# The opening of an FNet and channel-mix kernel: index patterns, transfers and float32 rows in another order, one angle operation on ScalarE, mu rows on VectorE

## The chip, the cores and the metric

The kernel runs on one core of a Trainium2 chip. The metric is the device time of one execution in microseconds (us). A core has five engines with instruction streams of their own: TensorE (PE in the profile; PEld is its weight load), VectorE (DVE), ScalarE (ACT), GpSimd (POOL) and SyncE (SP). They wait for each other through semaphores. Transfers are issued by SP, ScalarE and GpSimd on queues of their own and are carried out by 16 DMA engines.

## What is computed

`x` has 8 batches of 3072 rows of 256 numbers. The first half is the real part of a two-dimensional Fourier transform of each batch, the second a channel mix of that result with its own predecessor row:

```python
X = np.fft.fft(x, axis=1)
X = np.fft.fft(X, axis=2)
x = X.real
x_prev = np.concatenate([zeros, x[:, :-1, :]], axis=1)
xk = mu_k * x + (1.0 - mu_k) * x_prev
xr = mu_r * x + (1.0 - mu_r) * x_prev
k = np.maximum(xk @ w_k, 0.0)
v = k * k @ w_v
r = 1.0 / (1.0 + np.exp(-(xr @ w_r)))
return r * v
```

`w_k` is 256 x 1024, `w_v` 1024 x 256, `w_r` 256 x 256. Inputs and output are float32; the kernel computes in float16 with float32 sums.

## The kernel before

**The transform** is made of matmuls with tables of sines. A row and its mirror image in the batch have related coefficients, so the kernel first *folds*: `fold` (L160) adds rows read forwards (`xp`) to mirrored rows (`xm`) and writes `p` in float16, on VectorE. A batch has two halves: half 0 has nine slots of 96 rows (slot 0 by itself), half 1 has eight. `xp` comes by plain strided transfers (`load_p`, L129), which turn float32 into float16 on the way; `xm` comes by gathers (`load_m`, `load_m0`, L143 to L151), whose row numbers are in `idx_8`, `idx_4` and `idx_0`. These are patterns that GpSimd writes with `iota`. A gather is issued by GpSimd after its pattern is there. GpSimd's queue carries all transfers into SBUF but one: batch 0's first five slots, which SP loads as float32 into `xp_32` (L245) without a change of type.

**Batch 0** is the opening, since nothing runs before it. It folds in pieces: slots 1 to 4 of half 0, then slots 5 to 8, then half 1 in two pieces of four, then slot 0 (L900 to L916). `a_sum` (L616) multiplies each piece by the table `w_pm`, four matmuls of 208 columns per pair of slots; ScalarE or VectorE copies the sums out of PSUM into `a`. Then come the second factor (`d_units`, L643), a correction (`turned`, L685), the third factor with the table `m_cs` (`c_sums`, L704), and the mix with mu. The first matmuls of the channel mix are at L818.

**The tables** are made on the chip while the first rows are on their way: GpSimd writes `ramp` and `pcol_i`, VectorE makes rows from them, TensorE multiplies these into angles in PSUM, VectorE scales and reduces them (`ts`, L307, is its helper; `m_angles`, L430), and ScalarE takes the sine. `m_angles` writes `ang` for c = 0 and 1: a block of 32 columns and a block of 416 each, from PSUM to int32, then one AND over all 896. `m_sine` (L462) makes `m_cs` from it; `m_turned` (L466) copies it with a sign on VectorE. `w_pm` is written by ScalarE (L425, L427), and two operations of VectorE scale a part of it and make its negative (L894, L895).

**mu** is a row of 256 numbers for each of two uses. `mu_rows` (L255) puts it into the order that the kernel needs with three small copies on ScalarE; two small matmuls (L906) turn it into columns, which ScalarE copies into `muf_t`. The first mix and `turn_table` read them.

**Order.** Each engine runs its instructions in the order in which the program emits them; the last line, `pin_order`, fixes it. `keep_busy` (L232) fills waiting time of TensorE with matmuls of zeros; `NF` says how many in each place (`NF[0]` in front of the first `a_sum`). The weights `w_k` are gathered by `loads` (L475) behind the transfers of batch 0, with row numbers that `rows` (L271) writes on GpSimd.

Of the kernel before, what the change touches and what calls it, by code (L numbers as in the profile page):

```python
# [39 lines left out]
def kernel(  # L40
# [10 lines left out]
    nc = tc.nc  # L51
# [60 lines left out]
    p_sb = [const.tile([112, 256 * (9 - h) + 2], FP16, name=f"p{h}") for h in range(2)]  # L112
    xp_32 = const.tile([96, 5, 256], FP32)
    idx_4 = const.tile([96, 2], UINT32)
    idx_8 = const.tile([96, B, 2], UINT32)
    idx_0 = const.tile([96, B], UINT32)
    idx_g8 = const.tile([112, B, 2], UINT32)
# [10 lines left out]

    def load_p(b, h, q0=0):  # L129
        r, n = 9 * h + q0, 9 - h - q0  # L130
        if b > 1:
            for g in range(2):
                src = dataclasses.replace(x[b, 32 * g + r:32 * g + r + 1, :],
                                          ap=[[64 * D, N1], [D, n], [1, D]])
                nc.gpsimd.dma_start(out=xp_t[b, h][64 * g:64 * g + N1, 0:n], in_=src)
            return
        src = dataclasses.replace(x[b, r:r + 1, :], ap=[[32 * D, 96], [D, n], [1, D]])
        nc.gpsimd.dma_start(out=xp_t[b, h][0:96, q0:q0 + n], in_=src)

# [20 lines left out]
    def fold(b, h, q0=0, n=0):  # L160

        n = n or 9 - h
        if (b, h) not in p_t:
            p_t[b, h] = p_sb[h][:, 0:256 * (9 - h)].rearrange("p (q d) -> p q d", d=256)
        k = parts(b)
        p, xp, xm = p_t[b, h][0:k], xp_t[b, h][0:k], xm_t[b, h][0:k]
        o = XM0 + 256 * (8 - h - q0)
        if (b, h, q0) == (0, 0, 0):
            xm, o = xm_00, 1
        if (b, h) == (0, 0) and q0 < 5:  # L170
            xp = xp_32
        V.tensor_tensor(out=p[:, q0:q0 + n], in0=xp[:, q0:q0 + n],  # L172
                        in1=_v(xm, o + 256, [(-256, n), (-1, 256)]), op=ALU.add)
        V.tensor_tensor(out=p[:, q0:q0 + n, 0], in0=xp[:, q0:q0 + n, 0],
                          in1=_v(xm, o, [(-256, n)]), op=ALU.add)
# [56 lines left out]
    def keep_busy(n, ps, cols=512):  # L232

        for _ in range(n):
# [5 lines left out]
    keep_busy(1, fill, 384)  # L240
    NF = (14, 0, 1, 3, 0, 0, 0)

    nc.sync.dma_start(out=xp_32, in_=dataclasses.replace(x[0, 0:1, :],  # L245
                                                         ap=[[32 * D, 96], [D, 5], [1, D]]))
    mu_row = const.tile([2, 257], FP32)
# [7 lines left out]
    def mu_rows():  # L255
        nc.scalar.activation(out=mu_row[:, 256:257], in_=mu_row[:, 128:129], func=AF.Copy)
        for a in range(2):
            nc.scalar.activation(out=mu_p[:, a], in_=_v(mu_row, 256 * a, [(1 - 2 * a, 2),
                                                                         (2 - 4 * a, 64)]),
                                 func=AF.Copy)  # L260

    for h in range(2):
        x_tiles(0, h)
    load_p(0, 0, 5)
    for xm in xm_sb:
# [21 lines left out]
    iota(pcol_i, pattern=[[0, 1]], base=0, channel_multiplier=1)  # L287
    iota(idx_8, pattern=[[S // 8, B], [-1, 2]], base=S // 8 - 1, channel_multiplier=-4)
    iota(idx_4, pattern=[[-1, 2]], base=S // 4 - 3, channel_multiplier=-8)
    load_m(0, 0, 0, 8, idx_8[:, 0, 0:1])  # L290
    load_p(0, 1)
    load_m(0, 1, 1024, 4, idx_4[:, 0:1])
    load_m(0, 1, 0, 4, idx_4[:, 1:2])
    iota(idx_0, pattern=[[S, B]], base=S, channel_multiplier=-32)
    iota(idx_0[0:1], pattern=[[S, B]], base=0, channel_multiplier=0)
    rows()
    load_m0(0)

# [131 lines left out]
    def m_angles():  # L430
        for c in range(2):
            ts(ang[:, c, 0], ang_ps[:, 0:32], float(TURN) / S, MUL, ph_c[:, 2 * c + 1:2 * c + 2],
               ADD)
        rest = ang_ps[:, 32:32 * NJ]
        for c in range(2):
            ts(ang[:, c, 1:], rest, float(TURN) / S, MUL, ph_c[:, 2 * c:2 * c + 1], ADD)
        ts(ang, ang, TURN - 1, ALU.bitwise_and)

# [177 lines left out]
    def a_sum(b, h, i0, eng="A", m=4):  # L616
# [5 lines left out]
        for i in range(m):  # L622
            parts = [(h, i0 + i + 1 - h, 0, 2 * WA, 0, 1)]
            if h and i0 + i == 7:
                parts = [(0, 0, 0, WA, WA, 1), (1, 7, 1, WA, 1, 2)]
            for half, q, o, n, w, step in parts:
# [264 lines left out]


    mu_rows()
    ts(w_pm[:, 0:2, WA:WA + WB], w_pm[:, 0:2, WA:WA + WB], math.sqrt(0.5), MUL)  # L894
    ts(w_pm[:, 2], w_pm[:, 0], -1.0, MUL)  # L895
    m_sine()
# [5 lines left out]
    fold(0, 0, 5, 4)  # L902
    a_sum(0, 0, 4)
    mu_ps = ps_v()
    for a in range(2):
# [4 lines left out]
    nc.scalar.activation(out=muf_t, in_=mu_ps[:, 0:6], func=AF.Copy)  # L910
    m_turned()
    keep_busy(NF[2], ang_ps)
# [295 lines left out]
```

## Time and profile before

| | |
|---|---|
| median of 3 runs | 427.2 us (427.09 to 427.3) |
| the profiled execution | 427.09 us |
| its span, from the first to the last instruction | 425.3 us |
| granted TensorE clock, mean over the span | 1.000 |
| TensorE busy | 419.0 us (99%) |
| VectorE busy | 371.0 us (87%) |
| ScalarE busy | 325.8 us (77%) |
| GpSimd busy | 64.0 us (15%) |

The profile is of one execution. A page of it tells how long each engine was busy, the chain of work that ended last, and the costliest groups of instructions. Further views of the same trace are the timeline of an engine (start, length, engine, line, operation, output<-inputs, shape; in square brackets the idle time before it and what ended it), the chain in order of time, the groups by form, and the DMA queues in a stretch of time. L172 is line 172 of the kernel. The release of a wait is inferred from semaphores. For a transfer that GpSimd issues, the row on GpSimd is the time in which it writes the descriptors; the data move later.

### The profile page before, as it was taken

To read this page: it belongs to the slowest core of one execution; us is meant where nothing else is said; L and a number is where in the kernel's file an instruction comes from. 1 tells how busy PE (TensorE), PEld (TensorE's weight loads), DVE (VectorE), ACT (ScalarE), POOL (GpSimd) and SP (SyncE) were. 2 spreads that over 40 slices of the span, in tenths; PEclk is the share of its full clock that TensorE was granted. 3 is DMA by queue.
4 is the path that set the end of the run, shared out by engine and by line. 5 is a ranking of instruction groups with operands and counts; after the bars stand their busy time and mean duration, and the time that the engine had idled before them with its cause. 6 is when DMAs were issued, how large, how long until landed. Compare 5 with 4: busy or idle time off the path is not lost.

```text
span 425.3 us, 9647 instructions
## 1 busy us (share of the span) xinstructions
PE 419.0 (99%) x3992; PEld 294.1 (69%) x3992; DVE 371.0 (87%) x591; ACT 325.8 (77%) x406; POOL 64.0 (15%) x99
## 2 busy tenths in 40 slices
PE   8999999999999999999999999999999999999996
PEld 3667766776677767776767776777767766776765
DVE  8999999999998989989899898988899776977553
ACT  7889886797867986689767887678876798666661
POOL 7478500200060001400041000500000000000000
PEclk9999999999999999999999999999999999999999
DMA  8879962632385233932349232772323222332333
GB/s 171 111 114 201 229 148 55 116 90 55 70 160 137 54 75 56 219 96 51 76 77 218 57 71 58 135 167 62 70 57 76 55 63 60 74 72 53 76 76 99
DMA packets 35104, 42.08 MB, mean 99 GB/s; under 512 B 4114, under 2 KB 31092, under 8 KB 35060
## 3 DMA queue, kind: packets, MB, share of 16 engines
q1 hardware_dynamic: 27488, 25.41, 24.6%
q0 software_dynamic: 7264, 15.80, 21.7%
q8 instruction: 31, 0.51, 0.5%
q10 hardware_dynamic: 308, 0.26, 0.2%
q14 instruction: 13, 0.11, 0.1%
HBM read 32.08 MB, written 25.17 MB: 135 GB/s over the span
## 4 chain that ended last, share of the span: by engine, by line
PE 96%; DMA 1%; DVE 1%; issue 0%; POOL 0%; ACT 0%; POOLq 0%
PE psW L818 39%; PE psV L859 37%; PE psW L845 10%; PE psV L871 3%; PE psW L739 2%; PE psW L610 1%; DMA xm<-in_x_dram,idx 1%; PE psW L672 1%; PE psW L628 1%; PE psW L650 1%; DVE p L172 0%; PE psW L707 0%; PE psV L628 0%; PE psV L650 0%; PE psW L235 0%
## 5 line engine op out<-in xcount | busy, mean ns | idle before, releaser
L828 ACT ACTIVATE rl<-psW 128x1024 f16<-128x1024 f32 x192 | 193.7, 1031 | 82.3 <-PE psW L818 81.2
L818 PE MATMUL psW<-x,wk 128*128 128x512 f16 (+1 forms) x776 | 193.4, 377 | 0.3 <-DVE x L952 0.3
L859 PE MATMUL psV<-wv_sb,k 128*128 128x256 f16 x1424 | 184.3, 273 | 0.0
L859 PEld LDWEIGHTS <-k 128*128 128x128 f16 x1424 | 136.4, 98 | 38.3
L838 DVE TENSOR_TENSOR k<-rl 128x2048 f16<-128x2048 f16 (+1 forms) x100 | 115.6, 1156 | 26.3 <-ACT rl L828 26.0
L818 PEld LDWEIGHTS <-wk 128*128 128x128 f16 x776 | 75.6, 98 | 54.9 <-issue 0.4
L881 DVE SCALAR_TENSOR_TENSOR o<-psV,r 128x512 f32<-128x512 f32 (+1 forms) x97 | 65.8, 681 | 15.0 <-PE psV L859 14.1
L783 DVE TENSOR_TENSOR x<-y,t 128x1536 f16<-128x1536 f16 (+3 forms) x76 | 62.4, 827 | 2.2
L850 ACT ACTIVATE r<-psW 128x1024 f16<-128x1024 f32 x48 | 49.4, 1030 | 0.8 <-PE psW L845 0.8
L845 PE MATMUL psW<-wr,x 128*128 128x256 f16 x384 | 49.8, 273 | 0.0
L845 PEld LDWEIGHTS <-x 128*128 128x128 f16 x384 | 37.5, 98 | 14.2 <-issue 0.2
L567 ACT ACTIVATE g_all<-psW 128x512 f16<-128x512 f32 (+8 forms) x62 | 28.8, 538 | 1.3 <-PE psW L672 1.0
L567 ACT ACTIVATE a<-psW 128x832 f16<-128x832 f32 x31 | 25.4, 865 | 1.6 <-PE psW L610 1.2
L487 POOL IOTA gate<- 1x1 int32 x7 | 0.8, 121 | 162.5 <-DVE gate L486 162.5
L567 ACT ACTIVATE pq<-psW 128x1024 f16<-128x1024 f32 (+1 forms) x27 | 23.3, 916 | 1.5 <-PE psW L739 1.4
L141 POOL DMA_INDIRECT xm<-in_x_dram,idx_g x18 | 23.1, 1282 | 5.5 <-issue 5.5
L172 DVE TENSOR_TENSOR p<-xp,xm 112x2304 f16<-112x2304 f16 (+6 forms) x19 | 21.6, 1139 | 0.4 <-DMA xm<-in_x_dram,idx 0.4
L772 DVE TENSOR_SCALAR t<-d,muf_t 128x1536 f16<-128x1536 f16 (+3 forms) x44 | 21.9, 509 | 0.1
L772 DVE TENSOR_SCALAR t<-d,mu_m 128x1536 f16<-128x1536 f16 x32 | 19.6, 613 | 0.0
L752 DVE TENSOR_TENSOR y<-pq 128x960 f16<-128x960 f16 (+3 forms) x28 | 15.8, 606 | 3.2 <-ACT pq L567 2.8
L760 DVE TENSOR_TENSOR d<-y 128x1664 f16<-128x1664 f16 (+5 forms) x19 | 16.8, 882 | 0.3 <-ACT y L567 0.2
L871 PE MATMUL psV<-wv_sb,k 128*128 128x256 f16 x112 | 14.7, 273 | 0.0
(148 smaller groups left out, 217.4 us busy)
## 6 DMA issues: line engine op xcount, KB each, us to landing
out_dram<-o SPq DMA_DIRECT2D x189, 128.0 KB, 2.4
xp<-in_x_dram POOLq DMA_DIRECT2D x12, 216.0 KB, 4.3
xp<-in_x_dram POOLq DMA_DIRECT2D x13, 192.0 KB, 6.7
xp<-in_x_dram POOLq DMA_DIRECT2D x2, 384.0 KB, 6.8
wv_sb<-in_moe_w_v_dram POOLq DMA_DIRECT2D x1, 512.0 KB, 7.4
xp<-in_x_dram SPq DMA_DIRECT2D x1, 480.0 KB, 4.3
xp<-in_x_dram POOLq DMA_DIRECT2D x1, 432.0 KB
xm<-in_x_dram,idx_g POOLq DMA_INDIRECT x18, 8.2
```

What stands on the lines that cost most here:

```text
L141: nc.gpsimd.indirect_dma_start(dst, None, src, bass.IndirectOffsetOnAxis(ap=idx, axis=0))
L567: nc.scalar.activation(out=out_ap, in_=in_ap, func=AF.Copy)
L772: V.tensor_scalar(out=dst, in0=src, scalar1=mu, scalar2=None, op0=ALU.mult)
L783: V.tensor_tensor(out=_v(x_t[b, j, m], o, [(64 * step, hi - lo), (step, 64)]), in0=y_t[b][:, lo + 3 * m:hi + 3 * m, a], in1=x_t["t", a][:, ...
L818: nc.tensor.matmul(out=st["k", ds][:, 512 * hs + lo:512 * hs + hi], lhsT=wk_sb[m][a][:, 128 * fc:128 * fc + 128], rhs=xk[:, a, 512 * i + l ...
L828: nc.scalar.activation(out=st["rl"][:, 2 * ds:2 * ds + 2], in_=st["k", ds].rearrange("p (f t) -> p f t", f=2), func=AF.Relu, bias=0.0, sca ...
L838: V.tensor_tensor(out=k2_t[c][:, lo:hi], in0=r, in1=r, op=ALU.mult)
L845: nc.tensor.matmul(out=ps[:, 256 * tb:256 * tb + 256], lhsT=x_t[b, 1, m][:, a, 512 * i + 128 * tb: 512 * i + 128 * tb + 128], rhs=wr_sb[m] ...
L850: nc.scalar.activation(out=st["r", c], in_=ps, func=AF.Sigmoid)
L859: nc.tensor.matmul(out=st["v", tb - h][:, 256 * h:256 * h + 256], lhsT=k2_t[c][:, fc, 128 * tb:128 * tb + 128], rhs=wv_sb[:, fc], start=(f ...
L871: nc.tensor.matmul(out=st["v", tb - h][:, 256 * h:256 * h + 256], lhsT=k2_t[c][:, fc, 128 * tb:128 * tb + 128], rhs=wv_sb[:, fc], start=fc ...
L881: V.scalar_tensor_tensor(out=o.rearrange("p a b -> p (a b)")[:, 0:256 * n], in0=st["v", t0][:, 0:256 * n], scalar=16.0, in1=st["r", c][:, ...
```

## The change

It touches the opening alone.

1. **Which rows come as float32.** SP loads four slots (5 to 8) into `xp_32` instead of five (0 to 4). GpSimd loads slots 0 to 4 with the change of type instead of 5 to 8. So the fold of slots 1 to 4 reads float16, that of 5 to 8 float32, that of slot 0 float16.
2. **GpSimd's order.** Before: xp of half 0, `ramp`, `pcol_i`, `idx_8`, `idx_4`, gather of half 0, xp of half 1, two gathers of half 1, `idx_0` (two patterns), six row patterns, gather of slot 0. After: `ramp`, `pcol_i`, `idx_8`, xp of half 0, gather of half 0, xp of half 1, `idx_4`, first gather of half 1, `idx_0` (two patterns), second gather of half 1, gather of slot 0, six row patterns. `idx_8` and `idx_0` hold two batches instead of eight (4 and 2 columns instead of 16 and 8).
3. **Angles.** The 416-column operation of c = 1 goes from VectorE to ScalarE (Identity with scale and bias). The AND is split into two of 448 columns; between them stand the two operations on `w_pm`, which came behind the AND before.
4. **mu rows.** The three copies go from ScalarE to VectorE, and from in front of `m_sine` to behind the second fold and `m_turned`, in front of the first fold of half 1. `m_turned` keeps its place on VectorE.
5. **Filler and matmuls.** `NF[0]` is 12 instead of 14. In the last piece of half 1 the two matmuls that read slot 0 come behind the two that read half 1.

```diff
-    xp_32 = const.tile([96, 5, 256], FP32)
+    xp_32 = const.tile([96, 4, 256], FP32)
     idx_4 = const.tile([96, 2], UINT32)
-    idx_8 = const.tile([96, B, 2], UINT32)
-    idx_0 = const.tile([96, B], UINT32)
+    idx_8 = const.tile([96, 2, 2], UINT32)
+    idx_0 = const.tile([96, 2], UINT32)
...
-    def load_p(b, h, q0=0):
-        r, n = 9 * h + q0, 9 - h - q0
+    def load_p(b, h, n=0):
+        r, n = 9 * h, n or 9 - h
...
-        p, xp, xm = p_t[b, h][0:k], xp_t[b, h][0:k], xm_t[b, h][0:k]
+        p, xp, xm = p_t[b, h][0:k], xp_t[b, h][0:k, q0:], xm_t[b, h][0:k]
...
-        if (b, h) == (0, 0) and q0 < 5:
+        if (b, h, q0) == (0, 0, 5):
             xp = xp_32
...
-    NF = (14, 0, 1, 3, 0, 0, 0)
+    NF = (12, 0, 1, 3, 0, 0, 0)
...
-    nc.sync.dma_start(out=xp_32, in_=dataclasses.replace(x[0, 0:1, :],
-                                                         ap=[[32 * D, 96], [D, 5], [1, D]]))
+    nc.sync.dma_start(out=xp_32, in_=dataclasses.replace(x[0, 5:6, :],
+                                                         ap=[[32 * D, 96], [D, 4], [1, D]]))
...
     def mu_rows():
-        nc.scalar.activation(out=mu_row[:, 256:257], in_=mu_row[:, 128:129], func=AF.Copy)
+        V.tensor_copy(out=mu_row[:, 256:257], in_=mu_row[:, 128:129])
         for a in range(2):
-            nc.scalar.activation(out=mu_p[:, a], in_=_v(mu_row, 256 * a, [(1 - 2 * a, 2),
-                                                                         (2 - 4 * a, 64)]),
-                                 func=AF.Copy)
+            V.tensor_copy(out=mu_p[:, a], in_=_v(mu_row, 256 * a, [(1 - 2 * a, 2),
+                                                                   (2 - 4 * a, 64)]))
...
-    load_p(0, 0, 5)
...
     iota(ramp, pattern=[[1, P]], base=0, channel_multiplier=0)
     iota(pcol_i, pattern=[[0, 1]], base=0, channel_multiplier=1)
-    iota(idx_8, pattern=[[S // 8, B], [-1, 2]], base=S // 8 - 1, channel_multiplier=-4)
-    iota(idx_4, pattern=[[-1, 2]], base=S // 4 - 3, channel_multiplier=-8)
+    iota(idx_8, pattern=[[S // 8, 2], [-1, 2]], base=S // 8 - 1, channel_multiplier=-4)
+    load_p(0, 0, 5)
     load_m(0, 0, 0, 8, idx_8[:, 0, 0:1])
     load_p(0, 1)
+    iota(idx_4, pattern=[[-1, 2]], base=S // 4 - 3, channel_multiplier=-8)
     load_m(0, 1, 1024, 4, idx_4[:, 0:1])
+    iota(idx_0, pattern=[[S, 2]], base=S, channel_multiplier=-32)
+    iota(idx_0[0:1], pattern=[[S, 2]], base=0, channel_multiplier=0)
     load_m(0, 1, 0, 4, idx_4[:, 1:2])
-    iota(idx_0, pattern=[[S, B]], base=S, channel_multiplier=-32)
-    iota(idx_0[0:1], pattern=[[S, B]], base=0, channel_multiplier=0)
+    load_m0(0)
     rows()
-    load_m0(0)
...
         rest = ang_ps[:, 32:32 * NJ]
-        for c in range(2):
-            ts(ang[:, c, 1:], rest, float(TURN) / S, MUL, ph_c[:, 2 * c:2 * c + 1], ADD)
-        ts(ang, ang, TURN - 1, ALU.bitwise_and)
+        ts(ang[:, 0, 1:], rest, float(TURN) / S, MUL, ph_c[:, 0:1], ADD)
+        nc.scalar.activation(out=ang[:, 1, 1:], in_=rest, func=AF.Identity, bias=ph_c[:, 2:3],
+                             scale=float(TURN) / S)
+        ts(ang[:, 0], ang[:, 0], TURN - 1, ALU.bitwise_and)
+        ts(w_pm[:, 0:2, WA:WA + WB], w_pm[:, 0:2, WA:WA + WB], math.sqrt(0.5), MUL)
+        ts(w_pm[:, 2], w_pm[:, 0], -1.0, MUL)
+        ts(ang[:, 1], ang[:, 1], TURN - 1, ALU.bitwise_and)
...
-                parts = [(0, 0, 0, WA, WA, 1), (1, 7, 1, WA, 1, 2)]
+                parts = [(1, 7, 1, WA, 1, 2), (0, 0, 0, WA, WA, 1)]
...
-    mu_rows()
-    ts(w_pm[:, 0:2, WA:WA + WB], w_pm[:, 0:2, WA:WA + WB], math.sqrt(0.5), MUL)
-    ts(w_pm[:, 2], w_pm[:, 0], -1.0, MUL)
     m_sine()
...
     a_sum(0, 0, 4)
+    m_turned()
+    mu_rows()
     mu_ps = ps_v()
...
     nc.scalar.activation(out=muf_t, in_=mu_ps[:, 0:6], func=AF.Copy)
-    m_turned()
     keep_busy(NF[2], ang_ps)
```

More of the change, by code (lines that the diff above doesn't have):

```diff
@@ L137, in load_p @@
         src = dataclasses.replace(x[b, r:r + 1, :], ap=[[32 * D, 96], [D, n], [1, D]])
-        nc.gpsimd.dma_start(out=xp_t[b, h][0:96, q0:q0 + n], in_=src)
+        nc.gpsimd.dma_start(out=xp_t[b, h][0:96, 0:n], in_=src)
     def gather(dst, src, idx):
@@ L169, in fold @@
             xm, o = xm_00, 1
-        if (b, h) == (0, 0) and q0 < 5:
+        if (b, h, q0) == (0, 0, 5):
             xp = xp_32
-        V.tensor_tensor(out=p[:, q0:q0 + n], in0=xp[:, q0:q0 + n],
+        V.tensor_tensor(out=p[:, q0:q0 + n], in0=xp[:, 0:n],
                         in1=_v(xm, o + 256, [(-256, n), (-1, 256)]), op=ALU.add)
-        V.tensor_tensor(out=p[:, q0:q0 + n, 0], in0=xp[:, q0:q0 + n, 0],
+        V.tensor_tensor(out=p[:, q0:q0 + n, 0], in0=xp[:, 0:n, 0],
                           in1=_v(xm, o, [(-256, n)]), op=ALU.add)
```

## The prediction

> **What bounds the kernel now.** I read the page's shares and its chain first, then the chain of waits of the first 16 us, then the timelines of VectorE, GpSimd, TensorE and ScalarE over that stretch, and last the DMA view in narrow windows.
>
> ```profile
> PE 419.0 (99%) x3992; PEld 294.1 (69%) x3992; DVE 371.0 (87%) x591; ACT 325.8 (77%) x406; POOL 64.0 (15%) x99
> ...
> PE 96%; DMA 1%; DVE 1%; issue 0%; POOL 0%; ACT 0%; POOLq 0%
> ```
>
> TensorE carries 96% of the chain, so the other 4% is where an opening can gain. Of this chain, over the opening (start, length, what):
>
> ```profile
> 1.25 0.20 POOL xp L138
> ...
> 2.79 4.99 DMA xm<-in_x_dram,idx
> ...
> 7.81 1.23 DVE p L172
> ...
> 9.29 1.68 PE psW L628 x16
> ...
> 11.56 0.32 PE psV L235
> 11.88 0.73 PE psW L628 x8
> 12.61 1.05 PE psV L628 x10
> ...
> 18.01 1.03 PE psW L818 x8
> ```
>
> The mirrored rows of batch 0 (first gather) land at 7.79 and release the first fold. From 9.29 the chain names TensorE, though part of that is filler. VectorE shows what really ends last:
>
> ```profile
> 5.01 0.29 DVE L309 TENSOR_SCALAR ueo<-ueo 128x256 int32<-128x256 int32 x1
> 5.22 1.52 DVE L309 TENSOR_SCALAR rl<-psV,ph_c 128x32 int32<-128x32 f32 x4
> 6.77 0.63 DVE L309 TENSOR_SCALAR rl<-rl 128x896 int32<-128x896 int32 x1
> 7.32 0.42 DVE L309 TENSOR_SCALAR w_pm<-w_pm 128x104 f16<-128x104 f16 x2
> 7.81 1.22 DVE L172 TENSOR_TENSOR p<-xp,xm 96x1024 f16<-96x1024 f32 x1
> ...
> 9.94 0.44 DVE L309 TENSOR_SCALAR m_cs<-m_cs,sc 128x896 f16<-128x896 f16 x1
> 10.75 0.69 DVE L172 TENSOR_TENSOR p<-xp,xm 96x1024 f16<-96x1024 f16 x1 [0.37 <-DMA xm<-in_x_dram,idx]
> ```
>
> The first column is the start, the second the length. Two things to see. VectorE finished its table work at 7.32 + 0.42 = 7.74, just before the gather landed: both were critical at once. And the third fold, at 10.75, came after 0.37 us of waiting for the second gather. Its two halves feed the matmuls of 11.7 and 12.6, and from there every stage hangs on the one before, up to the first matmul of the channel mix at 18.01. So the change is worth what it moves that third fold; after that I count 1:1.
>
> **The gathers, the first term.** GpSimd issues its transfers in its own order (a DMA row is its descriptor work, not the transfer):
>
> ```profile
> 1.25 0.68 POOL L138 DMA_DIRECT2D xp<-in_x_dram  x1 [0.81 <-POOLq L1192]
> 2.02 0.28 POOL L286 IOTA ramp<- 128x128 int32 x1
> ...
> 2.29 0.22 POOL L288 IOTA idx<- 96x16 uint32 x1
> 2.43 0.17 POOL L289 IOTA idx<- 96x2 uint32 x1
> 2.79 1.01 POOL L141 DMA_INDIRECT xm<-in_x_dram,idx  x1 [0.19 <-DVE g_i L309]
> ...
> 4.67 0.95 POOL L141 DMA_INDIRECT xm<-in_x_dram,idx  x1 [0.30 <-issue]
> ...
> 11.53 0.94 POOL L141 DMA_INDIRECT wk<-in_moe_w_k_dram,row_i  x1 [0.30 <-issue]
> ```
>
> After the change GpSimd starts with three patterns. If they start at 1.25 as the DMA did: 0.1 for its set-up (1.93 to 2.02), 0.27 from the first to the third start (2.02 to 2.29), 0.17 for a third pattern of 4 columns (the row with 2 takes that), 0.1 to the DMA. The xp transfer is issued at 1.25 + 0.64 = 1.89, 0.64 later than now, and ends at 2.5; 0.30 of gap, and the first gather is issued at 2.8, as now. What the smaller and the later pattern save is spent on having xp between. If the patterns can start sooner (the profile doesn't explain the 0.81 of idle time before the DMA), all this is earlier; half of those 0.81, 0.4, is the most that I allow.
>
> What counts is when the data moves. SP's transfer (queue 1) and GpSimd's (queue 0) share the 16 engines. In the windows 1.2 to 3.6 and 3.6 to 4.4 us:
>
> ```profile
> q1 hardware_dynamic: 89, 0.46, 72.1%
> ```
> ```profile
> q0 software_dynamic: 58, 0.12, 78.3%
> q1 hardware_dynamic: 23, 0.04, 18.5%
> ```
>
> Queue 0 moved nothing until SP's rows were nearly through, although its xp was issued at 1.25. A later transfer of the same form met an empty queue: issued at 23.18, its first packets show at 24.6 in the window 23.8 to 25 (40 slices of 0.03 us, tenths of busy time):
>
> ```profile
> 23.18 0.67 POOL L138 DMA_DIRECT2D xp<-in_x_dram  x1
> ```
> ```profile
> DMA  0000000000000000000000009999909999000009
> ```
>
> So I read the late start of queue 0 as waiting behind SP, not as its own latency (then 1.4), and 0.64 us of later issue is covered: 1.89 + 1.4 = 3.3, about when SP's shorter transfer leaves the engines (four rows instead of five, 0.098 MB less at 0.46 MB in 1.8 us: 0.38 us sooner than 3.6). Against this, xp has five rows instead of four: 49 KB more at the rate of the full queue, here in the window 7.8 to 10.6:
>
> ```profile
> q0 software_dynamic: 250, 0.56, 105.6%
> ```
>
> that is 0.2 MB per us, so +0.25. Net -0.13; I take **-0.1** for the landing of both gathers (the second stands behind the first in a full queue). Bounds: the fold can't start before VectorE is ready. Its second 416-column operation goes to ScalarE (0.64 in the groups by form,
>
> ```profile
> L309 DVE TENSOR_SCALAR rl<-psV,ph_c 128x416 int32<-128x416 f32 x2 | 1.2, 644 | 0.0
> ```
>
> less 0.1 of overlap with its neighbour). The AND in two halves costs 0.1 to 0.2 more (0.63 for 896 columns, 0.29 for 256, so about 0.4 for 448, less overlap). VectorE is ready at 7.74 - 0.54 + 0.1 = 7.3, hence at best **-0.5**. At worst the cover is gone, which is the second rival: **+0.7**.
>
> **VectorE between the gathers, the second term.** From the first fold's start to the third's are 2.94 us, 0.37 of it waiting: 2.57 of work. The two first folds change types (float32 1.22 first becomes float16 0.68 first, float32 second): their sum stays. The mu rows come in, three small copies. ScalarE paid 0.18 and 0.51 for them:
>
> ```profile
> 5.93 0.18 ACT L256 ACTIVATE mu_row<-mu_row 2x1 f32<-2x1 f32 x1
> 6.02 0.51 ACT L258 ACTIVATE mu_p<-mu_row 2x128 f32<-2x128 f32 x2
> 7.43 1.04 ACT L463 ACTIVATE m_cs<-rl,sc 128x896 f16<-128x896 int32 x1 [0.90 <-DVE rl L309]
> ...
> 13.39 0.55 ACT L567 ACTIVATE a<-psV 128x416 f16<-128x416 f32 x1
> ```
>
> On VectorE the nearest copies (groups by form: mean ns of one) are
>
> ```profile
> L456 DVE COPY mu_m<-muf_t 128x2 f32<-128x2 f32 x2 | 0.3, 172 | 0.0
> ...
> L933 DVE COPY g<-g_all 128x127 f16<-128x127 f16 x1 | 0.2, 190 | 0.0
> ```
>
> Neighbours overlap by some 0.05 to 0.1, so three cost 0.25 to 0.55 (the last waits for the first); I take 0.4. Now 2.57 + 0.4 = 2.97 against a gather that comes 2.94 after the fold: **+0.03**, from 0 to +0.2. The wait of 0.37 hides the rest; if the second gather came sooner, this cover would be gone and the rows would cost up to 0.4. Behind them on VectorE stand the folds of half 1; TensorE's mu matmuls wait for them too, with a filler of 0.3 us (11.56 in the chain) behind them as slack.
>
> **What costs nothing, and its cover.** ScalarE's new angle operation (416 columns: a copy of that size takes 0.55, the sine of 896 columns from int32 1.04, so 0.5 to 0.7) stands where the mu rows were, 5.93 to 6.6, and VectorE wants it at about 6.9; if it were late, the last AND, the first fold and ScalarE's sine behind it would be. The sine starts at 7.3 instead of 7.43. TensorE's filler loses two of 14 matmuls:
>
> ```profile
> 4.95 3.69 PE L235 MATMUL psW<-zeros 128*128 128x512 f16 x14
> 9.29 1.68 PE L628 MATMUL psW<-w_pm,p 96*128 96x208 f16 x16 [0.66 <-DVE p L174]
> ```
>
> 0.4 less, in front of 0.66 of idle time: the first float16 fold ends 0.54 sooner, so the first eight matmuls start at about 8.7, the second eight wait for the float32 fold and end as now. The fold of slot 0 (now float16) and the swapped order of its matmuls end behind matmuls that ran without a gap: 0. The gather for slot 0 and the row patterns trade places; both stand before wk, whose second half was issued at 11.53 and takes
>
> ```profile
> wk<-in_moe_w_k_dram,row_i POOLq DMA_INDIRECT x2, 4.8
> ```
>
> so it lands at 16.3, 1.7 before its first use at 18.0.
>
> **The sum.** The profiled execution took 427.09 (span 425.3, and 1.8 around it). -0.1 + 0.03 = -0.07: 427.0. The median of the three runs is 0.1 higher, so I forecast **427.1**: no change within 0.2% (0.85 us), which is about what a measurement of this kernel can tell from none.
>
> **Rivals.**
> *The gathers land sooner.* GpSimd's patterns start right after the start barrier, the first gather is issued 0.4 earlier and its first packets no longer start late; VectorE is ready at 7.3. For it: the unexplained 0.81. Against it: the queue was full from 3.6 on, and bytes in front of the second gather are the same. -0.5 at the fold, but then the mu rows no longer hide entirely (+0.1): 426.8 by the rows. Only if the second gather, too, gains all that the engines stood idle in the window 1.2 to 3.6 (28% of 2.4 us, 0.7), and the forecast's own 0.1 on top, would it be 426.4, the edge of 0.2%.
> *Queue 0 starts late by itself (the other side).* The first transfer of GpSimd needs 3.6 - 1.25 = 2.4 us from issue to first packet whatever SP does. Then xp starts at 1.89 + 2.4 = 4.3, the engines idle before it, and the gather lands 0.64 later, plus 0.25 for the fifth row, minus 0.15 for SP's packets that no longer share (18.5% of 0.8): +0.7, and with the mu rows 427.9; with the extra row at its full price and the copies at 0.55, 428.2. It decides as soon as the first packet of queue 0 comes later than about 3.7. For it: nothing else in the trace is a first transfer. Against it: 1.4 at 23.18.
> The Trainium skill has a rule that would speak for this rival: by its page "DMA: Bandwidth & Descriptors", section "Queues, rings and completion order", an engine alternates between the queues it has work for, a packet at a time, so that a queue which is ready is not shut out. By that rule queue 0 would have been unready until 3.6, and the sum would be 427.9. The same section gives a packet as typically 9 to 17 descriptors; SP's 96 rows are 6 per engine, so one packet, and by that reading the trace agrees with my forecast.
> *VectorE takes over.* The copies wait on each other and cost 0.7 instead of 0.4: 2.57 + 0.7 is 0.33 over the gather: 427.5 - 0.1 = 427.4, still no change.
>
> **How the numbers follow.** Forecast 0.56, gathers sooner 0.20, queue 0 late 0.16, VectorE 0.08. Of the second I put 0.13 beyond 0.2% (how much the half-idle engines before 3.6 are worth is the cost that I can't bound better), of the third 0.11, its upper half and the cases where both it and the copies hit. Faster 0.13, same 0.76, slower 0.11. The range runs from the sooner gathers at their best, 426.4, to the late queue's middle, 428.0.
>
> **What would show it.** Right: the first fold is float16, about 0.69 long, and starts at 7.6 to 7.8; third fold at 10.6 to 10.8 with little or no wait for DMA; the first channel-mix matmul (L818 now) at 17.8 to 18.1. Late queue: the window 3.3 to 4.2 has no q0 packets, fold after 8.2. Sooner gathers: patterns before 1.2, fold at 7.3. Wrong altogether: the start of the first channel-mix matmul moves by more than 0.85, or time changes behind it, where I expect every stage to keep its length.

## The result and the profile after

| | before | after |
|---|---|---|
| median | 427.3 us (426.97 to 430.24, 21 runs) | 431.17 us (428.36 to 432.18, 21 runs) |
| ratio after to before | | 1.0074, 95% interval 1.0056 to 1.0091 |
| the profiled execution | 427.09 us, span 425.3 | 431.55 us, span 429.8 |
| mean granted TensorE clock of it | 1.000 | 0.989 |

The change made the kernel slower by 0.7%. The page of after, its shares, its clock in 40 slices and its chain:

```profile
PE 420.6 (98%) x3990; PEld 296.0 (69%) x3990; DVE 370.4 (86%) x594; ACT 326.3 (76%) x404; POOL 63.7 (15%) x99
...
PEclk9699999999999999999999999999999999999998
...
PE 96%; DMA 2%; DVE 1%; issue 0%; POOL 0%; ACT 0%; POOLq 0%; DVEq 0%
```

Two things are new: the second of the 40 slices has 6 tenths of the clock (before, all have 9), and DMA has 2% of the chain instead of 1%. Both lie in the opening. Its chain of waits (start, length, what):

```profile
1.42 0.72 POOL xp L138
2.14 0.30 issue
2.44 6.96 DMA xm<-in_x_dram,idx
...
9.51 0.70 DVE p L172
...
11.79 1.57 PE psW L631 x8
...
16.28 1.73 PE psV L631 x10
...
22.36 1.03 PE psW L821 x8
```

The first gather is issued at 2.44, 0.35 sooner than before, and takes 6.96 us instead of 4.99. It lands at 9.40 instead of 7.79. The first channel-mix matmul starts at 22.36 instead of 18.01, 4.35 later. Behind it nothing changed: 429.8 - 22.36 = 407.4, before 425.3 - 18.01 = 407.3. VectorE's timeline of after:

```profile
7.09 0.39 DVE L308 TENSOR_SCALAR rl<-rl 128x448 int32<-128x448 int32 x1
9.51 0.69 DVE L172 TENSOR_TENSOR p<-xp,xm 96x1024 f16<-96x1024 f16 x1 [2.02 <-DMA xm<-in_x_dram,idx]
...
12.00 0.13 DVE L256 COPY mu_row<-mu_row 2x1 f32<-2x1 f32 x1
12.07 0.39 DVE L258 COPY mu_p<-mu_row 2x128 f32<-2x128 f32 x2
12.70 0.69 DVE L172 TENSOR_TENSOR p<-xp,xm 96x1024 f16<-96x1024 f16 x1 [0.25 <-issue]
```

GpSimd's:

```profile
0.85 0.23 POOL L284 IOTA ramp<- 128x128 int32 x1 [0.40 <-POOLq L1193]
...
1.42 0.72 POOL L138 DMA_DIRECT2D xp<-in_x_dram  x1 [0.16 <-issue]
2.44 0.97 POOL L141 DMA_INDIRECT xm<-in_x_dram,idx  x1 [0.30 <-issue]
```

And TensorE's:

```profile
4.61 2.75 PE L235 MATMUL psW<-zeros 128*128 128x512 f16 x12
10.46 0.98 PE L631 MATMUL psW<-w_pm,p 96*128 96x208 f16 x8 [3.10 <-DVE p L174]
11.79 1.57 PE L631 MATMUL psW<-w_pm,p 96*128 96x208 f16 x8 [0.34 <-DVE p L174]
```

VectorE is ready at 7.48, sooner than before, and then waits 2.02 us for the gather. TensorE runs out of fillers at 7.36 and idles for 3.10 us. Then two equal groups of eight matmuls take 0.98 and 1.57. The windows say why (time, length, busy time of PE, PEld, DVE, ACT and POOL, granted clock, DMA share, GB/s; cut where the trace records a change of the clock, and every 3.41 us from there):

```profile
4.29:7.70 3.41, 3.07 (x15) 1.21 (x13) 3.06 (x13) 2.29 (x6) 2.76 (x5) 1.00 1.00 153
7.70:11.11 3.41, 0.65 (x8) 0.65 (x8) 1.57 (x3) 3.04 (x6) 2.73 (x9) 1.00 1.03 192
11.11:14.52 3.41, 3.06 (x18) 2.15 (x16) 3.06 (x11) 1.86 (x3) 1.23 (x1) 0.50 1.02 169
14.52:17.94 3.42, 3.42 (x20) 2.94 (x19) 0.52 (x3) 1.42 (x4) 1.85 (x4) 0.50 0.37 44
17.94:21.35 3.41, 3.07 (x43) 1.99 (x43) 2.79 (x10) 2.02 (x5) 0.00 (x0) 1.00 1.08 146
```

Before, the stretch with the least work in front of the channel mix was this:

```profile
5.95:9.36 3.41, 2.75 (x14) 1.05 (x13) 3.23 (x8) 2.47 (x9) 2.97 (x10) 1.00 1.03 202
```

After a stretch of 3.41 us in which TensorE was busy for only 0.65, its clock is granted at 0.50 for two such stretches, 11.11 to 17.94, just where the sums of the opening stand. The 4.35 us split by two rows of the timeline: the third fold starts at 12.70 instead of 10.75 (+1.95), and from there to the first channel-mix matmul it is 9.66 us instead of 7.26 (+2.40). So there are two causes to test: a late gather and a lowered clock.

### The profile page after: what moved, and what is told of

It is laid out like the page before. It is cut to its first block, busy times and chain, and to the rows that moved or that the text cites. A ratio compares the mean times of both kernels' runs of the same rounds, so it can differ in the third digit from the quotient of the medians.

```text
span 429.8 us, 9646 instructions
## 1 busy us (share of the span) xinstructions
PE 420.6 (98%) x3990; PEld 296.0 (69%) x3990; DVE 370.4 (86%) x594; ACT 326.3 (76%) x404; POOL 63.7 (15%) x99
## 4 chain that ended last, share of the span: by engine, by line
PE 96%; DMA 2%; DVE 1%; issue 0%; POOL 0%; ACT 0%; POOLq 0%; DVEq 0%
PE psW L821 39%; PE psV L862 37%; PE psW L848 10%; PE psV L874 3%; DMA xm<-in_x_dram,idx 2%; PE psW L742 2%; PE psW L613 1%; PE psW L675 1%; PE psW L631 1%; PE psW L653 1%; DVE p L172 0%; PE psV L631 0%; PE psW L710 0%; PE psV L653 0%; PE psV L908 0%
```

## The experiments

Each run lists its mean clock. One stretch of 3.41 us at half clock takes 0.004 off it, so I count a run as lowered below 0.997. (The clock also falls behind TensorE's last work at the end of every profile; where this lies inside the span it takes up to 0.003 off.) "SP" is the number of rows of x (one for each slot) that SP's transfer brings to a partition, "xp" its place on GpSimd against the three patterns `ramp`, `pcol_i`, `idx_8`, "F" is `NF[0]`. The next four columns are of one profiled execution: start of the first fold, of the third fold, of the first channel-mix matmul, and time at half clock. Before was run beside every experiment; its row counts the 153 runs of all five rounds together; its runs that aren't lowered have medians of 427.19 to 427.31 in the five.

| kernel | SP | xp | F | fold 1 | fold 3 | mix | half clock | lowered runs | median | median, not lowered |
|---|---|---|---|---|---|---|---|---|---|---|
| before | 5 | ahead | 14 | 7.81 | 10.75 | 18.01 | 0 | 62 of 153 | 427.66 | 427.26 |
| after | 4 | behind | 12 | 9.51 | 12.70 | 22.36 | 6.83 | 17 of 21 | 431.17 | 428.64 |
| e1_order | 5 | behind | 14 | 8.28 | 11.20 | 18.45 | 0 | 2 of 12 | 427.61 | 427.49 |
| e2_rows | 4 | ahead | 14 | 7.96 | 10.80 | 19.70 | 3.41 | 5 of 12 | 428.43 | 427.23 |
| e3_tables | 5 | ahead | 14 | 8.33 | 11.66 | 18.83 | 0 | 3 of 12 | 427.66 | 427.56 |
| e4_filler | 4 | behind | 22 | 9.98 | 13.36 | 21.90 | 3.41 | 1 of 12 | 429.69 | 429.67 |
| e5_order_tables | 5 | behind | 12 | 8.03 | 11.24 | 21.06 | 6.83 | 9 of 12 | 429.71 | 427.77 |
| e6_order_rows | 4 | behind | 14 | 9.17 | 11.91 | 20.86 | 3.41 | 11 of 12 | 431.58 | 428.51 (1 run) |
| e7_split_row | 4 | behind | 12 | 9.66 | 12.85 | 22.50 | 6.83 | 9 of 9 | 431.45 | |
| e8_few_fillers | 5 | ahead | 4 | 7.88 | 10.86 | 21.64 | 10.24 | 12 of 12 | 430.97 | |
| e9_sp_five | 5 | behind | 12 | 8.30 | 11.47 | 20.05 | 3.41 | 5 of 12 | 428.23 | 428.08 |
| e10_sp_four_low | 4 | behind | 14 | 9.19 | 12.19 | 20.82 | 3.41 | 8 of 12 | 430.49 | 428.19 |
| e11_before_16 | 5 | ahead | 16 | 7.83 | 10.75 | 18.03 | 0 | 1 of 12 | 427.31 | 427.27 |
| e12_gather_first | 5 | behind gather | 16 | 7.63 | 12.55 | 22.26 | 6.83 | 12 of 12 | 431.15 | |
| e13_patterns_between | 4 | behind | 12 | 9.49 | 12.82 | 19.99 | 0 | 9 of 12 | 430.24 | 428.68 |
| e14_sp_five_18 | 5 | behind | 18 | 8.77 | 11.94 | 19.10 | 0 | 1 of 12 | 428.03 | 428.02 |
| e15_mu_on_scalar | 5 | behind | 18 | 8.01 | 10.74 | 18.03 | 0 | 0 of 12 | 427.91 | 427.91 |
| e16_xp_first | 4 | ahead | 12 | 8.01 | 11.17 | 21.05 | 6.83 | 9 of 12 | 430.13 | 427.65 |
| e17_best | 4 | ahead | 18 | 7.81 | 10.58 | 18.05 | 0 | 1 of 12 | 427.72 | 427.65 |

### The parts of the change alone

`e1_order` is the kernel before with GpSimd's new order and smaller patterns, `e2_rows` with the other rows in float32 (and the swapped matmuls of the last piece), `e3_tables` with the angle and mu edits alone:

```diff
 # e1_order
-    load_p(0, 0, 5)
...
-    iota(idx_8, pattern=[[S // 8, B], [-1, 2]], base=S // 8 - 1, channel_multiplier=-4)
+    iota(idx_8, pattern=[[S // 8, 2], [-1, 2]], base=S // 8 - 1, channel_multiplier=-4)
+    load_p(0, 0, 5)
...
 # e2_rows
-    nc.sync.dma_start(out=xp_32, in_=dataclasses.replace(x[0, 0:1, :], ap=[[32 * D, 96], [D, 5], [1, D]]))
+    nc.sync.dma_start(out=xp_32, in_=dataclasses.replace(x[0, 5:6, :], ap=[[32 * D, 96], [D, 4], [1, D]]))
...
 # e3_tables
-        for c in range(2):
-            ts(ang[:, c, 1:], rest, float(TURN) / S, MUL, ph_c[:, 2 * c:2 * c + 1], ADD)
+        ts(ang[:, 0, 1:], rest, float(TURN) / S, MUL, ph_c[:, 0:1], ADD)
+        nc.scalar.activation(out=ang[:, 1, 1:], in_=rest, func=AF.Identity, bias=ph_c[:, 2:3], scale=float(TURN) / S)
```

> The kernel before with GpSimd's new order and the smaller patterns alone (rows, tables and filler as before). Theory 'order' (the first gather lands late because its xp is issued just ahead of it, behind the patterns): first fold starts at 8.9 to 9.5 as in the changed kernel, ratio 1.003 to 1.010. Theory 'rows' (late because GpSimd's first transfer carries five rows): fold at 7.8 or sooner, since the gather is issued at 2.44 instead of 2.79, ratio 0.999 to 1.000.

> The kernel before with the other rows in float32 alone: SP loads slots 5 to 8, GpSimd slots 0 to 4, in GpSimd's old order. Theory 'order': gather at 7.8 as before, ratio 0.999 to 1.000. Theory 'rows': the 16 engines finish the gather far apart, fold at 8.9 to 9.5, ratio 1.003 or more, 1.009 where the clock falls too.

> The kernel before with the table edits alone: angle operation on ScalarE, the split AND, mu rows on VectorE. Theories 'order' and 'rows': gather at 7.8; the mu rows take about 0.4 where 0.37 was waited, ratio 1.000 to 1.0005. Rival 'VectorE locks GpSimd out' (the new 32-bit operations delay GpSimd's descriptors): fold after 8.5, ratio 1.002 or more.

Ratios 1.0005 (0.9981 to 1.0029), 1.0012 (0.9978 to 1.0046) and 1.0008 (0.998 to 1.0037): none of the parts alone makes the loss, and none moves the first fold beyond 8.33, so neither "order" nor "rows" is right by itself. The late gather needs two of them together. `e3_tables` lies between its two theories (8.33, against 7.8 and after 8.5); its transfers are those of before, so half a microsecond at the first fold (8.33 against 7.81) can also lie between two executions with the same transfers.

### The fillers and the clock

`e4_filler` is the changed kernel with 22 fillers, `e8_few_fillers` the kernel before with 4, `e11_before_16` the kernel before with 16.

```diff
-    NF = (12, 0, 1, 3, 0, 0, 0)    # the changed kernel
+    NF = (22, 0, 1, 3, 0, 0, 0)    # e4_filler
...
-    NF = (14, 0, 1, 3, 0, 0, 0)    # the kernel before
+    NF = (4, 0, 1, 3, 0, 0, 0)     # e8_few_fillers
+    NF = (16, 0, 1, 3, 0, 0, 0)    # e11_before_16
```

> The changed kernel with 22 instead of 12 filler matmuls in front of the first sums. Theory 'clock' (TensorE idles 3.1 us while it waits for the gather, and its clock is halved for 6.8 us after that): the clock stays at 1.00, all runs are at 428.2 to 429.0, ratio 1.002 to 1.004; what is left is the late gather. Rival 'gather alone' (the chain waits for transfers anyway, so the halved clock costs nothing): ratio stays at 1.007 to 1.010 although the clock is full.

> The kernel before with 4 instead of 14 filler matmuls of zeros in front of the first products: TensorE idles about 3.2 us there, with transfers and folds as before. Theory 'the idle time lowers the clock': a granted clock of 0.50 in one or two stretches of 3.41 us between 10 and 18 us in most runs, first fold still at 7.8, first channel-mix matmul at 19.3 to 21, ratio 1.003 to 1.007, i.e. 1.2 to 3 us by the clock alone. Rival 'fillers cost and are worth nothing' (as I priced them at first): first channel-mix matmul at 18.0, clock 1.000, ratio 0.999 to 1.001.

> The kernel before with 16 instead of 14 fillers in front of the first products: 0.66 us of idle time becomes about 0.1. Clock theory: of its runs fewer than the 24 of 60 of the kernel before have a clock below 0.997; median 427.1 to 427.5, mean below that of before, first channel-mix matmul at 18.0. Rival (the lowered clock of before has nothing to do with this idle time): a share near 0.4, same median and mean.

`e8_few_fillers` settles what idle time of TensorE is worth: transfers and folds are those of before, yet the ratio is 1.0054 (1.0032 to 1.0076). Its windows:

```profile
4.42:7.83 3.41, 1.30 (x6) 0.39 (x4) 3.21 (x12) 2.39 (x8) 2.72 (x6) 1.00 1.06 184
7.83:11.24 3.41, 1.87 (x11) 1.65 (x12) 2.89 (x6) 3.09 (x7) 2.79 (x7) 0.50 1.05 194
11.24:14.65 3.41, 3.41 (x20) 2.61 (x18) 2.10 (x7) 1.64 (x3) 1.72 (x4) 0.50 0.80 115
14.65:18.07 3.42, 3.42 (x18) 2.35 (x17) 0.84 (x2) 1.37 (x3) 1.13 (x3) 0.50 0.97 124
```

A stretch with 1.30 us of work is followed by three at half clock, and the first channel-mix matmul comes at 21.64, 3.6 us later, more than the 1.2 to 3 that I had expected. The table gives the price: from the third fold to the first channel-mix matmul are 7.16 to 7.47 us in the seven experiments at full clock, 8.54 to 8.95 in the five with one halved stretch, 9.65 to 9.88 in the five kernels with two, 10.78 with three.

In the changed kernel more fillers (`e4_filler`) leave 1 of 12 runs lowered, but the median only falls to 429.69 (ratio 1.0037, 1.0017 to 1.0057), above the 428.2 to 429.0 that I had expected: the gather is still late. It is also 1.0 above the four runs of the changed kernel that aren't lowered, 428.64. Those may be the ones whose gather was less late, or the fillers may cost something; which, isn't shown. `e11_before_16` makes it likely that the kernel before loses runs to the same cause: 1 of 12 lowered, against 14 of 34 of before in the same round and 62 of 153 in all. Its ratio of 0.999 (0.9963 to 1.0018) can't be told from none; its mean is 427.8, that of the 153 runs of before 428.3.

### Which two parts make the gather late

`e5_order_tables` is the changed kernel with the old rows in float32, `e6_order_rows` the changed kernel without the angle and mu edits (and with 14 fillers), `e7_split_row` the changed kernel with GpSimd's xp transfer cut to slots 1 to 4 and slot 0's row in a transfer of its own, just ahead of slot 0's gather:

```diff
 # e7_split_row
-    load_p(0, 0, 5)
+    load_p(0, 0, 4, 1)
...
+    load_p(0, 0, 1)
     load_m0(0)
```

> The changed kernel with the old rows (SP loads slots 0 to 4 as float32, GpSimd four slots of half 0): new order, table edits and filler of 12. Theory 'rows with order' (the first gather lands 1.6 us late because GpSimd's five-row transfer now stands right in front of it with no instructions between): with four rows the gather is nearly prompt, first fold at 7.8 to 8.4, first channel-mix matmul at 18.0 to 18.8, ratio 0.998 to 1.002. Rival 'order with tables' (the rows have no part in it; the earlier VectorE and ScalarE work disturbs GpSimd's descriptor writing): first fold at 8.9 to 9.6, TensorE idle 2.5 us or more in front of it, clock below 0.997 in most runs, ratio 1.004 to 1.010.

> The changed kernel without the table edits (all angle operations on VectorE, mu rows on ScalarE as before, filler of 14): new order and new rows. Theory 'rows with order': first gather lands at 9.0 to 9.9, first fold at 9 to 10, ratio 1.004 to 1.009; with two more fillers the clock is lowered less often than in the changed kernel. Rival 'order with tables': the gather is prompt, fold at 7.8 to 8.4, ratio 0.998 to 1.003.

> The changed kernel, but GpSimd's five-row transfer is cut: slots 1 to 4 (four rows, as before) stand in front of the first gather, slot 0's row is a transfer of its own just in front of slot 0's gather. Theory 'rows with order', through the length of the transfer: the first gather lands at 7.2 to 8.3, the first fold starts there, third fold at 10.2 to 11.2, clock 1.000, ratio 0.996 to 1.001. Rival (any transfer with change of type right in front of the gather makes it late once the rows in float32 are the later ones, or the tables do it): first fold at 8.9 to 9.6, ratio 1.003 to 1.009.

Order and rows make it (fold at 9.17, with the tables as before, so the rival that VectorE's and ScalarE's new work disturbs GpSimd falls too); order and tables don't (8.03), though with 12 fillers the clock still falls. The length of GpSimd's transfer, my explanation, is refuted: cut to four rows, the fold comes at 9.66. What is left of the rows is SP's side, four rows instead of five, or which rows they are. `e9_sp_five` is the changed kernel with SP loading rows 4 to 8 (row 4 is loaded twice), `e10_sp_four_low` is `e1_order` with SP loading rows 1 to 4 and slot 0's row by a later transfer:

```diff
 # e9_sp_five
-    nc.sync.dma_start(out=xp_32, in_=dataclasses.replace(x[0, 5:6, :], ap=[[32 * D, 96], [D, 4], [1, D]]))
+    nc.sync.dma_start(out=xp_32, in_=dataclasses.replace(x[0, 4:5, :], ap=[[32 * D, 96], [D, 5], [1, D]]))
...
 # e10_sp_four_low
-    nc.sync.dma_start(out=xp_32, in_=dataclasses.replace(x[0, 0:1, :], ap=[[32 * D, 96], [D, 5], [1, D]]))
+    nc.sync.dma_start(out=xp_32[:, 1:5], in_=dataclasses.replace(x[0, 1:2, :], ap=[[32 * D, 96], [D, 4], [1, D]]))
...
+    nc.gpsimd.dma_start(out=xp_32[:, 0:1], in_=dataclasses.replace(x[0, 0:1, :], ap=[[32 * D, 96], [D, 1], [1, D]]))
     load_m0(0)
```

> The changed kernel, but SP's transfer is five rows long again (rows 4 to 8; row 4 is loaded twice and its float32 copy not used). Theory 'short head': in the changed kernel SP's transfer leaves the engines sooner, GpSimd's queue begins on some engines earlier than on others, and the gather's share runs apart; with five rows the gather lands within 1.3 us of its first engine, at 7.6 to 8.4, and the first fold starts by 8.5; ratio 1.001 to 1.004 (the idle time of TensorE stays about 2 us with 12 fillers, so the clock is still lowered in many runs). Rival 'which rows' (the addresses that SP and GpSimd read beside each other): first fold at 9 to 10, engines 2 us or more apart, ratio 1.006 to 1.010.

> The kernel before with GpSimd's new order, SP loading four rows (1 to 4) instead of five, slot 0's row in float32 by a later GpSimd transfer; the rows in float32 stay the old ones. Theory 'short head': the gather's engines finish 2 us or more apart, first fold at 9 to 10, ratio 1.003 to 1.009. Rival 'which rows': as with the new order alone, fold at 7.8 to 8.4, ratio 0.999 to 1.003.

One more row for SP, which nobody reads, brings the fold from 9.51 to 8.30:

```profile
8.30 0.69 DVE L172 TENSOR_TENSOR p<-xp,xm 96x1024 f16<-96x1024 f16 x1 [0.81 <-DMA xm<-in_x_dram,idx]
```

and the median from 431.17 to 428.23 (ratio to before 1.0009, 0.9982 to 1.0035). Four low rows make it late (9.19; ratio 1.003, 1.0002 to 1.0058). So it is the length of SP's transfer that counts with the order, not which rows it brings. (Whether it is that four rows leave the engines sooner or that their packets are shorter isn't separated.) Queue 0 in the window 4.8 to 7.2 us (packets, MB, share of the 16 engines), in the changed kernel:

```profile
q0 software_dynamic: 104, 0.35, 90.3%
```

and in `e9_sp_five`, with the same times of issue:

```profile
q0 software_dynamic: 145, 0.47, 106.3%
```

The engines move a quarter less here. That isn't what the late kernels have in common: before moved 0.42 MB in this window, and `e13_patterns_between` below, with a fold at 9.49, as much:

```profile
q0 software_dynamic: 128, 0.42, 99.2%
```

What they share is that the engines drift apart. The trace has completion events of the engines' parts of the first gather (some are missing): these lie at 7.25 to 7.79 before, at 7.08 to 9.40 after, at 7.01 to 8.20 in `e9_sp_five`; in `e10_sp_four_low` all but one are there by 8.06 and the last comes at 9.16. In the six kernels with four rows for SP and xp behind the patterns the first and the last of these events are 2.1 to 2.7 us apart, in the other thirteen 1.64 at most. GpSimd's descriptor work isn't it: its rows for xp and the gather take 0.72 and 0.97 in the changed kernel and in `e9_sp_five`.

The order was split next. `e13_patterns_between` is the changed kernel with `idx_4` and `idx_0` written between GpSimd's xp transfer and the first gather; `e16_xp_first` is the changed kernel with the xp transfer in front of the patterns, as before:

```diff
 # e13_patterns_between
+    iota(idx_4, pattern=[[-1, 2]], base=S // 4 - 3, channel_multiplier=-8)
+    iota(idx_0, pattern=[[S, 2]], base=S, channel_multiplier=-32)
+    iota(idx_0[0:1], pattern=[[S, 2]], base=0, channel_multiplier=0)
     load_m(0, 0, 0, 8, idx_8[:, 0, 0:1])
...
 # e16_xp_first
+    load_p(0, 0, 5)
     iota(ramp, pattern=[[1, P]], base=0, channel_multiplier=0)
     iota(pcol_i, pattern=[[0, 1]], base=0, channel_multiplier=1)
     iota(idx_8, pattern=[[S // 8, 2], [-1, 2]], base=S // 8 - 1, channel_multiplier=-4)
-    load_p(0, 0, 5)
```

> The changed kernel with the patterns idx_4 and idx_0 written between GpSimd's xp transfer and the first gather, so the gather is issued at 2.8 to 2.9 as in the kernel before, with SP's four rows. Theory 'issue time': the gather then lands by 8.3 with its engines within 1.2 us, first fold by 8.4, ratio 1.000 to 1.004. Rival (the issue time has no part in it): fold at 9 to 10, ratio 1.006 to 1.010.

> The changed kernel with one line moved: GpSimd's xp transfer in front of the three patterns again. Theory 'xp behind the patterns': the gather's engines finish within 1 us, the first fold starts at 7.5 to 8.2, full-clock runs at 427.4 to 428.0; with 12 fillers TensorE still idles some 1.5 us, so the clock is lowered in part of the runs; ratio 0.999 to 1.004. Rival (any of the other parts): fold at 9 to 10, full-clock runs at 428.4 to 428.9, ratio 1.005 to 1.010.

Issued at 2.75 in `e13_patterns_between`, the gather is as late as when issued at 2.44, and by chance this execution kept its clock:

```profile
9.49 0.69 DVE L172 TENSOR_TENSOR p<-xp,xm 96x1024 f16<-96x1024 f16 x1 [2.15 <-DMA xm<-in_x_dram,idx]
...
12.82 0.69 DVE L172 TENSOR_TENSOR p<-xp,xm 96x1024 f16<-96x1024 f16 x1 [0.39 <-issue]
```

Its first channel-mix matmul starts at 19.99, 1.98 later than before: this is the price at full clock of the late gather (1.68 at the first fold) and of the longer way to the third fold, where the copies for mu are (3.33 instead of 2.94). By the medians of the runs that aren't lowered it is less, 1.4 (428.64 after and 428.68 here against 427.26). With the xp transfer ahead of the patterns (`e16_xp_first`, issued at 1.25 instead of 1.42) the first fold is at 8.01, and 427.65 is the median of its runs that aren't lowered, against those 428.64 and 428.68; each of these three is over 3 or 4 runs only. All six profiled kernels with four rows for SP and xp behind the patterns start the first fold at 9.17 or later, the others at 8.77 or sooner. `e16_xp_first` is no faster for it: 9 of 12 runs lowered, ratio 1.0022 (0.9994 to 1.005). Its windows:

```profile
5.35:8.76 3.41, 2.55 (x12) 0.97 (x10) 2.60 (x9) 2.72 (x5) 2.86 (x6) 1.00 0.99 197
8.76:12.18 3.42, 2.68 (x23) 1.95 (x23) 3.16 (x10) 3.37 (x8) 2.72 (x8) 1.00 0.96 161
12.18:15.59 3.41, 3.40 (x19) 2.94 (x20) 1.43 (x6) 1.38 (x3) 1.33 (x4) 0.50 0.84 135
```

Here no wait is longer than 1.06 us, and the clock still falls, after 2.68 of 3.41 us at work.

### Versions with both causes gone

`e12_gather_first` (old rows, the gather ahead of xp, 16 fillers) was a try at something faster. `e14_sp_five_18` is `e9_sp_five` with 18 fillers, `e15_mu_on_scalar` the same with the copies for mu on ScalarE in front of the sine, `e17_best` is `e16_xp_first` with 18 fillers and those copies on ScalarE.

```diff
 # e12_gather_first, against e5_order_tables
-    NF = (12, 0, 1, 3, 0, 0, 0)
+    NF = (16, 0, 1, 3, 0, 0, 0)
...
-    load_p(0, 0, 5)
     load_m(0, 0, 0, 8, idx_8[:, 0, 0:1])
+    load_p(0, 0, 5)
...
 # e15_mu_on_scalar and e17_best
-        V.tensor_copy(out=mu_row[:, 256:257], in_=mu_row[:, 128:129])
+        nc.scalar.activation(out=mu_row[:, 256:257], in_=mu_row[:, 128:129], func=AF.Copy)
...
+    mu_rows()
     m_sine()
...
     m_turned()
-    mu_rows()
```

> A try at a better version: the changed kernel with the old rows in float32, the first gather issued in front of GpSimd's xp transfer, and 16 fillers. If the gather lands by 7.4, VectorE (ready at 7.5) folds at once and the third fold, bound by the second gather, starts at 10.5 to 10.9: 426.9 to 427.6, clock mostly 1.000. Rival: queue 0's first transfer stays behind SP's, the gather lands at 7.5 to 8.3 and nothing is won: 427.4 to 428.5.

> The changed kernel with SP's five rows and 18 fillers: the prompt gather and no idle time of TensorE above 0.5 us. If the late gather and the clock are all of the loss but 0.7 us: median 427.9 to 428.3, clock above 0.997 in at least 10 of 12 runs, first channel-mix matmul at 18.5 to 19. Rival (the clock is lowered whatever the fillers do, by slower stages behind): 4 or more of 12 below 0.997, median as with 12 fillers, 428.2, or above.

> As e14_sp_five_18, with the copies for mu back on ScalarE in front of the sine. If the rest is the copies on VectorE: third fold 0.3 to 0.5 sooner, median 427.4 to 427.7. Rival (the second gather decides, as my sum for VectorE had it): third fold and median as in e14_sp_five_18 within 0.15.

> As e16_xp_first, with 18 fillers and the copies for mu on ScalarE. If both causes are gone: first fold 7.5 to 7.9, clock above 0.997 in at least 10 of 12 runs, median 426.9 to 427.4, and a mean 0.5 or more below that of the kernel before (428.2). If not: as e15_mu_on_scalar, 427.9, or above.

`e12_gather_first` gets its first fold at 7.63, but then xp is late (it releases the second fold, at 9.28), the third fold starts at 12.55 after a wait of 1.63 for which the trace names no releaser, and every run is lowered: 431.15, ratio 1.0059 (1.0037 to 1.0081). The gather's place at the head of the queue only moved the loss.

With both causes gone the loss is gone: ratios 0.9994 (0.9971 to 1.0017), 0.999 (0.9968 to 1.0012) and 0.9979 (0.995 to 1.0008). None can be told from before, so no version was shown to beat it; `e17_best`, at 427.72, misses the 426.9 to 427.4 that I had expected. `e15_mu_on_scalar` has the third fold 1.20 sooner than `e14_sp_five_18`, 0.76 of it from a first fold that came sooner in this execution; its median is only 0.12 lower, so what the copies on VectorE are worth in time isn't shown by this pair. `e17_best` has the earliest third fold of all, 10.58, and its first channel-mix matmul at 18.05 is no sooner than before. It also ends at a span of 426.0, 407.95 behind that matmul instead of 407.3; all three versions with 18 fillers, and `e4_filler` with 22, lose these 0.6 us at one place. There a group of eight matmuls with `wv_sb` and its waits takes 1.44 us (39.99 to 41.43 in `e15_mu_on_scalar`) instead of 0.87. Why, isn't shown.

## Why the prediction was wrong

**The step "TensorE's filler loses two of 14 matmuls", "0.4 less, in front of 0.66 of idle time", failed.** It priced idle time of TensorE at nothing. The granted clock was 1.000 in the one profile that I had, and I didn't ask what keeps it there. The runs show it: with 4 fillers instead of 14 and nothing else changed, the median of that round rises by 3.1 us (430.97 against 427.9) and the first channel-mix matmul of the profile by 3.6. In the profile of the changed kernel this is 2.40 of 4.35 us. The two fillers are the smaller part of it: with 14 and the late gather (`e6_order_rows`) 11 of 12 runs are lowered, not fewer as I had expected. The idle time of 3.10 comes mostly from the late gather, and the prediction's own worst case for the gather had no price for that either.

**The gathers term failed: -0.1 forecast, with +0.7 as the worst, +1.61 measured** (landing at 9.40 instead of 7.79). Its inputs were right or too cautious. The patterns started at 0.85, as the rival with sooner gathers had it, not at 1.25; the gather was issued at 2.44, not 2.8; and SP's shorter transfer did let queue 0 in sooner. In the window 3.2 to 3.6, where queue 0 had moved nothing before:

```profile
q0 software_dynamic: 12, 0.03, 51.8%
q1 hardware_dynamic: 19, 0.04, 37.8%
```

The rival of a queue 0 that is late by itself needed no packets of it until after 3.7, so it is refuted, though one of its signs, a fold after 8.2, came true. By the rule that it drew on, in the Trainium skill's "DMA: Bandwidth & Descriptors", section "Queues, rings and completion order" (an engine alternates between ready queues, a packet at a time), queue 0 need not wait for queue 1; this trace doesn't decide on it, since both move in that window. What failed is the step from bytes and issue times to a landing time: it took the 16 engines as one queue with a rate of 0.2 MB per us, and a gather lands with its last engine, here 2.3 us behind the first instead of 0.5. At full clock this already leaves the range: 428.64 is the median of the four runs that aren't lowered. The cause on the side of the program is shown (four rows for SP with xp behind the patterns); why some engines are late then is open.

**The VectorE term was mis-sized: +0.03 forecast, about +0.25 measured.** The copies take 12.00 to 12.46, 0.46 against my 0.4, and VectorE's work from the first fold to their end is 2.95, as in my sum (2.97). But the third fold starts 0.24 later still, after a pause that the trace puts down to no wait (`0.25 <-issue`; 0.18 to 0.21 in `e5_order_tables`, `e9_sp_five`, `e14_sp_five_18` and `e16_xp_first`), and the wait of 0.37 that should hide the copies was not there. From first to third fold are 2.94 us before, 3.16 to 3.21 in six kernels with the copies and the changed order (9.51 to 12.70 here, 8.01 to 11.17 in `e16_xp_first`), 3.33 and 3.38 in two more (`e13_patterns_between`, `e4_filler`; `e12_gather_first` aside), and 2.73 and 2.77 when ScalarE makes them (`e15_mu_on_scalar`, `e17_best`). The prediction had this case in half a sentence ("this cover would be gone and the rows would cost up to 0.4") and counted it at 0.1 in one rival.

**"After that I count 1:1" held at full clock and failed without it.** In `e13_patterns_between` the third fold is 2.07 late and the channel mix 1.98; after, 1.95 became 4.35.

**What was right:** the fold in float16 comes first and takes 0.69; ScalarE's angle operation takes 0.61 (0.5 to 0.7 forecast) and delays nothing on the path; the swapped matmuls and the gather for slot 0 show no cost (427.23 and 427.49 in the runs of `e2_rows` and `e1_order` that aren't lowered, 427.26 before); every stage behind the opening kept its length. "No change" would have been near for the program without its two side effects, 428.03 in `e14_sp_five_18`, just outside my range.

## What to carry to other kernels

Fillers of zeros are part of the timing: if an edit leaves TensorE waiting longer, add fillers with it, and price the wait by the stage that follows it at half clock. When transfers of several queues meet at the start, look at each engine's completion, not only at bytes, rate and issue times; two edits that are harmless alone need a run together. A profile at clock 1.000 doesn't show that the next execution has it: list the clock of many runs before reading a difference of a per cent.

## What the runs showed of the hardware

The clock was granted at 1.00 or 0.50 in the windows here, and the halved time came in lengths of 3.41, 6.83 and 10.24 us. The Trainium skill's "TensorE: Matmul & The Clock Gate", Part 1, gives half rate after an idle window of about 3.4 us in a grid that runs free of the program. The lengths agree. That the window must be idle does not: all eleven lowerings in the openings of these profiles followed a stretch with TensorE busy for 0.61 to 2.71 of its 3.41 us. No stretch with 2.74 or more was followed by one. Seven with 1.74 to 2.59 weren't either, so busy time by itself doesn't decide. The same program gets its clock lowered in some executions: 62 of 153 runs of the kernel before, with a median of 429.9 against 427.26. The grid lies otherwise in every profile (a stretch begins at 5.95 before, at 4.27 in `e11_before_16`), which may be why; no run shows it.

A transfer that is one row shorter made another one 1.2 us later (9.51 against 8.30 for the fold; 9.17 to 9.98 in the six kernels with four rows and xp behind the patterns, 8.01 to 8.77 in the five with five), although it has less to move and leaves the engines sooner (its last packet starts at 3.71 instead of 4.25). In the records of the changed kernel single packets of queue 0 of 4 KB, which mostly take some 0.3 us, take up to 1.5 us longer, between 4.4 and 7.7 us; before, at most 0.6 longer. What holds them was not found.
